# Sequence DFT summed apart over odd and even rows, and x loaded by row gathers, in an FNet-mixing and squared-ReLU kernel

## Chip, cores, metric

The kernel runs on one core of one Trainium2 chip. The metric is the device time of one execution, in microseconds (us). A "run" below is one kernel executed a few times beside the kernel before on the same chip. "Span" is the length of the one profiled execution, which is one or two us shorter than the time.

Engines are named as in the profile: PE (TensorE, the matmuls), DVE (VectorE), ACT (ScalarE), POOL (GpSimd) and SP (SyncE, which here only issues transfers, "DMAs"). SBUF is the on-chip memory, PSUM the one that the matmuls write.

## The reference

```python
x: (8, 3008, 256) f32;  w_in: (256, 2048);  w_out: (2048, 256)
X = fft(x, axis=1); X = fft(X, axis=2); a = X.real            # (8, 3008, 256)
h = maximum(a.reshape(-1, 256) @ w_in, 0)
return (h * h) @ w_out                                        # (24064, 256) f32
```

The real part of the two-dimensional DFT needs a cosine and a sine sum over the 3008 rows (the sequence DFT). Both kernels fold x first: rows n and 3008-n, n and 1504-n are added or subtracted, so that each sum runs over about 752 rows, held as 127 partitions times 6 values of q. The DFT over the 256 columns is multiplied into w_in once (G1, G2, G3).

## The kernel before: the parts that the change touches

x of one batch lies in one buffer. Half of it is needed in reversed row order. Eight large loads and two small ones go through the SP queue, which also carries the output stores and the edge rows:

```python
def down_rows(r0):                       # reversed half: slowest dimension is 3
    return bass.AP(tensor=x.tensor, offset=x.offset + r0 * D,
                   ap=[[PG * NQ * D, 3], [-NQ * D, PG], [1, NQ * D]])
def load_x(b):
    r = b * S
    for h in range(3):
        n0 = 1 + PG * NQ * (2 - h)
        for s in range(2):
            nc.sync.dma_start(out=x4[h*PG:(h+1)*PG, s, :, :], in_=up_rows(r + s*M + n0))
    for s in range(2):
        nc.sync.dma_start(out=x4[0:NP, 2 + s, :, :],
                          in_=down_rows(r + s*M + M - NQ - PG*NQ*2))
    ...                                  # two small loads of single rows
```

The 1505 frequencies of a batch are cut into four blocks. Every block takes 6 cosine and 6 sine matmuls (one for each q) of 376 columns, and 6 more for one "edge" row of features, done for one or two batches at a time:

```python
BLK = [(0, 377), (377, 376), (753, 376), (1129, 376)]
# one group, sn = 0 cosine, 1 sine:
mm(ps, w[0:KR, odd, q, :], cosT[0:KR, q, c0:c0+n], q == 0, q == NQ-1)     # x6
if q == NQ - 1:
    nc.scalar.copy(d[0:hi, c0:c0+n], ps[0:hi, :])
```

The main loop has 384 steps (48 chunks of 256 frequencies, 8 steps each). A step does 6 matmuls into xb (G1, G2, G3), two ReLUs on ACT, two squares on VectorE (DVE) and 8 matmuls of the previous chunk into po. The folds and the DFT of later batches are spread among the steps. In the profile lines xb and po are the PSUM tiles of the two products, r the ReLUs, h their squares, os output rows that wait to be stored, pt and qt the cosine and sine sums of a batch. The edge row is the cosine sum of the one feature (column 128) that the pairing of columns leaves over; it is made in tile es and copied by DMA into the last row of qt. Batch 0 is done ahead of the loop:

```python
alloc_pq(0); tables(0)
for f in fold_ops(0): f()                # ends with load_x(1)
gmats()
for f in stage1_ops(0, [0]) + e_ops([0], [0]): f()
for blk in (1, 2, 3):
    tables(blk)
    for f in stage1_ops(0, [blk]) + e_ops([0], [blk]): f()
```

## Time and profile before

| before | us |
|---|---|
| time, median of 3 | 832.75 (831.94 to 832.84) |
| span of the profiled run, mean granted clock | 831.6, 0.947 |
| first xb matmul (end of the head) | 98.6 |
| steps of batch 0 end (step 40) | 191.4 |

The last two rows come from the timeline of PE. They cut the span into three stages: the head (to the first xb matmul), batch 0's stage (40 steps, five chunks; the sixth already holds frequencies of batch 1) and the rest (344 steps).

The table by windows of the kernel before follows. The columns are the window and its length, then busy us (and instructions) of PE, PE weight loads, DVE, ACT and POOL, then the granted clock, the DMA share, and GB/s.

```profile
core 0: us, PE busy (x) PEld busy (x) DVE busy (x) ACT busy (x) POOL busy (x), PEclk, DMA share, GB/s
125.00:130.00 5.00, 5.00 (x44) 4.22 (x43) 0.00 (x0) 2.05 (x4) 0.00 (x0) 1.00 0.20 80
130.00:135.00 5.00, 0.57 (x6) 0.36 (x4) 0.00 (x0) 0.00 (x0) 0.00 (x0) 0.76 0.19 79
135.00:140.00 5.00, 0.00 (x0) 0.00 (x0) 2.02 (x5) 0.00 (x0) 0.00 (x0) 0.50 0.15 56
140.00:145.00 5.00, 4.32 (x20) 2.75 (x20) 5.00 (x13) 3.63 (x7) 0.00 (x0) 0.50 0.12 32
...
400.00:500.00 100.00, 98.42 (x925) 86.36 (x924) 51.50 (x138) 77.53 (x138) 0.00 (x0) 1.00 0.21 61
```

From 400 to 500 us PE is nearly always busy at full clock, so there PE is the bound. From 130 to 135 us no engine works for more than 0.6 us, while DMA moves only 79 GB/s at a share of 0.19, which is 3 of 16 engines. When PE starts again it has half the clock.

The timeline of the SP queue and of DVE, kernel before, shows what was awaited. Columns: start, us, engine, line, operation, tiles; in brackets the idle time before it and its releaser.

```profile
107.17 2.47 SPq L82 DMA_DIRECT2D x_96<-in_x_dram  x6
109.68 1.59 SPq L84 DMA_DIRECT2D x_96<-in_x_dram  x2
111.31 7.99 SPq L87 DMA_DIRECT2D x_96<-in_x_dram  x1
119.35 0.58 SPq L88 DMA_DIRECT2D x_96<-in_x_dram  x1
120.03 6.41 SPq L402 DMA_DIRECT2D out_dram<-os  x4
...
137.98 1.29 DVE L242 TENSOR_TENSOR u<-x_96 127x510 f16<-127x510 f32 x2 [14.31 <-DMA x_96<-in_x_dram]
```

x was asked for at 107.17 us and used at 137.98: 30.8 us for 3.08 MB. The small load at L87 held the queue for 8 us, and the stores (L402) stood behind it. During its 14.3 us wait for x DVE did nothing else. The squares that PE needs stand behind this fold in its program: they came at 139.2 us, ACT waited 12.6 us for them, and PE began again at 140.7.

### The profile page before, as it was taken

The page shows a single profiled execution, that of the slowest core. Times are in us where ns is not written, and L with a number is a line of the kernel's source. Part 1 is how long each engine was busy: PE and PEld are TensorE (multiplying, and loading weights), DVE is VectorE, ACT ScalarE, POOL GpSimd, SP SyncE. Part 2 cuts the span into 40 slices and gives each one's busy share as a digit, 9 for nine tenths or more (in the row PEclk, how much of TensorE's full clock was granted, in tenths as well). Part 3 has the DMA queues.
Part 4 walks back from the last instruction along what each step waited for, and adds up shares of the span by engine and source line. Part 5 has one row for each costly group of instructions (what it writes and reads, how often), then busy time and mean ns, then how long its engine had stood idle before and what let it go on. Part 6 is the DMA issues. An engine that isn't in the chain of part 4 may idle for free.

```text
span 831.6 us, 15590 instructions
## 1 busy us (share of the span) xinstructions
PE 709.7 (85%) x6200; PEld 580.1 (70%) x6200; DVE 403.7 (49%) x1097; ACT 558.6 (67%) x1008; POOL 11.4 (1%) x15
## 2 busy tenths in 40 slices
PE   0134595979999996979999995979999999999998
PEld 0012273848888975848888984847888988779887
DVE  3588573524444655423444655523444673334542
ACT  1535672746888864657778864646888887768884
POOL 5000000000000000000000000000000000000000
PEclk9995796989999997999999997989999999999999
DMA  9241041510111244311111243311111111101111
GB/s 176 72 111 41 2 115 68 139 63 32 39 39 39 72 119 114 107 42 39 39 39 39 63 122 108 113 49 39 34 44 40 40 39 39 36 29 41 51 39 52
DMA packets 35306, 52.57 MB, mean 63 GB/s; under 512 B 4034, under 2 KB 31202, under 8 KB 35234
## 3 DMA queue, kind: packets, MB, share of 16 engines
q1 hardware_dynamic: 32082, 49.49, 20.5%
q0 software_dynamic: 3152, 2.10, 1.8%
q8 instruction: 48, 0.79, 0.4%
q14 instruction: 24, 0.20, 0.1%
HBM read 29.00 MB, written 24.64 MB: 65 GB/s over the span
## 4 chain that ended last, share of the span: by engine, by line
PE 63%; DMA 18%; SPq 8%; DVE 7%; ACT 2%; issue 1%; POOL 1%; DVEq 0%; ACTq 0%; POOLq 0%
PE po L64 31%; PE xb L64 23%; DMA out_dram<-os 11%; DMA x_96<-in_x_dram 6%; PE pf L64 6%; SPq L87 4%; PE pe L64 3%; DVE u L242 2%; SPq L82 1%; SPq L84 1%; DVE tm L200 1%; DVE tt L203 1%; DMA qt<-es 1%; POOL x_96 L75 1%; SPq L88 1%
## 5 line engine op out<-in xcount | busy, mean ns | idle before, releaser
L435 ACT ACTIVATE r<-xb 128x512 f16<-128x512 f32 (+1 forms) x384 | 226.7, 591 | 134.3 <-PE xb L64 107.2
L446 ACT ACTIVATE r<-xb 128x512 f16<-128x512 f32 (+1 forms) x384 | 226.7, 590 | 25.4 <-PE xb L64 6.7
L64 PE MATMUL xb<-qt,G_199 128*128 128x256 f16 (+8 forms) x880 | 190.0, 259 | 2.0 <-DMA qt<-es 2.0
L64 PE MATMUL xb<-pt,G_198 128*128 128x256 f16 (+8 forms) x880 | 190.5, 260 | 0.6
L64 PE MATMUL xb<-qt,G_200 128*128 128x256 f16 (+8 forms) x880 | 148.4, 261 | 39.4 <-ACT r L435 39.4
L64 PEld LDWEIGHTS <-G_200 128*128 128x128 f16 x880 | 82.2, 99 | 50.4 <-issue 41.0
L64 PEld LDWEIGHTS <-G_198 128*128 128x128 f16 x880 | 83.9, 98 | 28.7 <-issue 16.9
L64 PEld LDWEIGHTS <-G_199 128*128 128x128 f16 x880 | 81.2, 98 | 19.7 <-issue 2.3
L376 ACT ACTIVATE os<-po 128x512 f32<-128x512 f32 (+1 forms) x95 | 56.3, 593 | 44.8 <-DMA out_dram<-os 40.8
L64 PE MATMUL pf<-cosT,w 127*128 127x376 f16 (+1 forms) x192 | 55.7, 344 | 24.0 <-ACT cosT L204 24.0
L64 PEld LDWEIGHTS <-w 127*127 127x127 f16 (+1 forms) x384 | 47.5, 126 | 39.5 <-issue 32.0
L64 PE MATMUL pf<-sinT,w 127*127 127x376 f16 (+1 forms) x192 | 55.2, 353 | 0.0
L242 DVE TENSOR_TENSOR u<-x_96 127x510 f16<-127x510 f32 x48 | 31.1, 685 | 46.5 <-DMA out_dram<-os 23.8
L64 PE MATMUL pe<-cosT,eall 127*2 127x376 f16 (+3 forms) x120 | 30.7, 361 | 9.4 <-ACT es L337 9.4
L64 PE MATMUL pc<-win_108,cosD 128*128 128x512 f16 x8 | 4.3, 615 | 30.7 <-DVE cosD L178 17.3
L204 ACT ACTIVATE cosT<-tt,bcos,tneg 128x376 f16<-128x376 f32 (+1 forms) x24 | 16.8, 699 | 15.4 <-DVE tt L203 15.4
L64 PEld LDWEIGHTS <-eall 127*2 127x2 f16 (+1 forms) x120 | 7.3, 86 | 24.4 <-issue 22.9
L64 PEld LDWEIGHTS <-cosD 128*128 128x128 f16 x8 | 1.0, 126 | 33.3 <-DVE cosD L178 19.4
L258 DVE TENSOR_TENSOR w<-v 127x381 f16<-127x381 f16 x64 | 20.7, 355 | 0.0
L311 ACT CAST qt<-pf 127x376 f16<-127x376 f32 (+1 forms) x32 | 15.3, 478 | 7.2 <-PE pf L64 7.2
L251 DVE TENSOR_TENSOR v<-u 127x512 f16<-127x512 f16 x48 | 18.6, 419 | 0.1
L311 ACT CAST pt<-pf 128x376 f16<-128x376 f32 (+1 forms) x32 | 15.4, 481 | 3.6 <-PE pf L64 3.4
(253 smaller groups left out, 1182.6 us busy)
## 6 DMA issues: line engine op xcount, KB each, us to landing
out_dram<-os SPq DMA_DIRECT2D x157, 128.0 KB
x_96<-in_x_dram SPq DMA_DIRECT2D x48, 252.0 KB
x_96<-in_x_dram SPq DMA_DIRECT2D x16, 756.0 KB
win_108<-in_moe_w_in_dram POOLq DMA_DIRECT2D x4, 256.0 KB, 13.8
wout_113<-in_moe_w_out_dram POOLq DMA_DIRECT2D x1, 1024.0 KB, 34.6
x_96<-in_x_dram SPq DMA_DIRECT2D x16, 2.0 KB
out_dram<-os SPq DMA_DIRECT2D x2, 108.0 KB
out_dram<-os SPq DMA_DIRECT2D x2, 104.0 KB
```

Of the source, the lines that this page charges most:

```text
L64: nc.tensor.matmul(o, l, r, start=start, stop=stop, skip_group_check=True)
L75: nc.gpsimd.memset(x4[96:128, :, :, :], 0.0)
L82: nc.sync.dma_start(out=x4[h * PG : (h + 1) * PG, s, :, :], in_=up_rows(r + s * M + n0))
L87: nc.sync.dma_start(out=t[:, 0 : NQ + 1 : NQ], in_=x[b : b + 1, 0 : M + 1 : M])
L204: nc.scalar.activation(cosT[:, q, c0 : c0 + n], t, AF.Sin, bias=bcos[:, q : q + 1], scale=tneg[:, q : q + 1])
L242: vt(u[k, :, q, 1:D], x4[k, 0:2, q, 1:D], x4[k, 3:1:-1, NQ - 1 - q, D - 1 : 0 : -1], op=ALU.add)
L251: vt(v[k, s, q : q + 2, :], u[k, 0, q : q + 2, :], u[k, 1, q : q + 2, :], op=ALU.subtract if s else ALU.add)
L258: vt(w[k, i, q : q + 3, 0 : P - 1], v[k, s, q : q + 3, 1:P], v[k, s, q : q + 3, D - 1 : P : -1], op=ALU.add if i < 2 else ALU.subtract)
L311: nc.scalar.copy(d[0:hi, c0 : c0 + n], ps[0:hi, :])
L376: nc.scalar.activation(os_[0:m, 0 : len(grp), :], st["o"][0:m, 0 : len(grp), :], AF.Copy, bias=0.0, scale=HS * HS)
L435: nc.scalar.activation(r[:, 0, :, 0:n], xb[:, :, 0:n], AF.Relu)
L446: nc.scalar.activation(r[:, 1, :, 0:n], xb[:, :, 0:n], AF.Relu)
```

## The change

The change has two parts and a new schedule that they allow.

1. For the lower half of the frequencies of each parity, odd and even rows are summed apart: A over even q, B over odd q. Then A+B is one frequency and the difference is its mirror image. So two blocks of 376 columns do the work of four. Each group costs 3+3 matmuls, one ACT copy of A to SBUF, and two DVE operations for sum and difference. Half the tables are needed. Edge rows are done for three and four batches at a time; those of batch 0 go into extra matmuls of its own groups.
2. x lies on the partitions in plain order; the reversed half is fetched by indirect DMA (a gather fetches 126 pieces of two rows, 2 KB each) on the GpSimd queue.
3. Only the first half of batch 0 is done ahead of the loop. The second half of its tables and its DFT go into steps 1 to 16, and the folds of batches 1, 2 and 3 into batch 0's steps.

```diff
+    def gather(b, s, part):
+        r0 = b * S + (s + 1) * M - NQ * NP + 2 * part
+        nc.gpsimd.indirect_dma_start(
+            out=x4[0:NP, 2 + s, 2 * part : 2 * part + 2, :].rearrange("p q d -> p (q d)"),
+            out_offset=None,
+            in_=bass.AP(tensor=x.tensor, offset=x.offset, ap=[[2 * D, B * S // 2], [1, 2 * D]]),
+            in_offset=bass.IndirectOffsetOnAxis(ap=idx[0:NP, 0:1], axis=0),
+            element_offset=r0 * D)
     def load_x(b):
-        ...                                     # 6 + 2 + 2 loads, nc.sync
         for s in range(2):
+            nc.gpsimd.dma_start(out=x4[0:NP, s, :, :], in_=up(b, s, 0, NQ))
+            for part in range(NQ // 2):
+                gather(b, 1 - s, part)
+        load_mid(b, nc.gpsimd)
-    BLK = [(0, 377), (377, 376), (753, 376), (1129, 376)]
+    BLK = ((0, HE), (HE, HO))                   # 377, 376 columns
...
+    # dft_ops: even q into one PSUM tile, odd q into another, then
+    act(st["a"], st[0], AF.Copy, ...)           # A to SBUF
+    vt(lo_, a, bp, op=ALU.add)                  # lower frequencies
+    vt(hi_, bp, a, op=ALU.subtract)             # mirrored ones (cosine)
...
-    alloc_pq(0) ... four rounds of tables, stage1, e_ops
+    for f in table_ops(0) + fe: f()             # fe: even half of the fold
+    for c in range(F // 512): gmat(c)
+    for f in stage1_ops(0, 0, True): f()
+    spread(fo, 1, 5)
+    spread(table_ops(1), 4, 10)
+    spread(stage1_ops(0, 1, True), 10, 16)
+    FOLD = {0: [1, 2, 3], 1: [4], 2: [5], 3: [6, 7]}
+    EGRP = {0: [1, 2, 3], 3: [4, 5, 6, 7]}
```

## The prediction

> **What bounds it now.** In undisturbed stretches PE does: the table by windows gives 400 to 500 us PE busy 98.4 of 100 us with 925 matmuls at clock 1.00, about 106 ns per 256-column matmul, so PE is at its rate; ACT is busy 78 us and DVE 52 us there. The rest is lost elsewhere. (a) The first xb matmul starts at 98.7 us (chain of waits): x is waited for until 40 us, then three rounds of tables, sequence DFT and edge DFT run in series. (b) Six pauses in which PE runs dry (about 130, 171, 310, 353, 501 and 541 us; roughly 43 us with the restarts, where the windows show clock 0.5). They come from x: the timeline of DVE shows it blocked 14.3 us before the fold at 138 us, and other chain pieces of 18 to 31 us are one x load landing. While the tail of a load arrives, the windows show a DMA share of 0.20 at 80 GB/s, about 3 of 16 engines. This agrees with the Trainium skill, "DMA: Bandwidth & Descriptors", section "Why a DMA increments its semaphore by 16 and not by 1": the engine count divides the slowest dimension, and the reversed load's slowest dimension is 3. The groups also show 6.8 us in issuing one small x row (L87), behind which output stores queue.
>
> **What the change does.**
> - Removes 276 matmuls of about 376 columns (192 sequence DFT, 84 edge DFT). At full rate one costs an estimated 0.16 us (from the 106 ns per 256 columns). 222 lie inside the PE-bound loop: -35 us.
> - Head: half the tables, no 5.2 us memset before x, x gathered by all engines, second half of the first batch's tables and DFT moved into the loop. Estimate: small vectors until 11 us, six table rounds of 2 us until 23, x by then, even folds (about 7 us) until 31, G and 18 DFT matmuls until 41. First xb at about 41 us: -57 us.
> - Adds per DFT group an ACT copy (half as many as before) and two VectorE sums of about 0.45 us (estimated from 0.41 to 0.61 us for 376-column f32 operations). ACT falls slightly, DVE rises some 10 to 15 us in all; neither becomes the bound in steady state (ACT 1.18 us of relus in a step of about 1.6 us).
> - Loads: 3.08 MB at the 187 GB/s seen when 16 engines run is 16.5 us (estimate), instead of about 31 us. Issue is off the store queue, onto an idle GpSimd.
> - New crowding: batch 0's steps now hold 12 us of tables and three folds. DVE there has an estimated 77 us of work in 40 steps, plus two waits of 4 to 8 us, as loads 2 and 3 are asked for only about 10 us ahead. So this stage is bound by DVE and x, ends at about 130 us (before: 194 us).
>
> **Sum.** 130 us to step 40; the remaining 344 steps took 638 us, of which about 37 are pauses; 600 - 33 (fewer matmuls) + 5 (batch 7's load) = 572. About 700 us; range 682 to 724. Chances: faster 0.97, same 0.02, slower 0.01.
>
> **What would show it.** First xb near 41 us; chunk 5 near 130; pauses after 150 us gone or under 5 us; 5924 matmuls, PE near 100% busy at clock 1.0, step about 1.65 us; x loads of 15 to 20 us with a DMA share well over 0.20; no long L87-like issues.
>
> **What would make it wrong.** Gathers slow to generate on GpSimd, or starved by DVE: each extra 10 us of load costs about 25 us in all. A loss of granted clock when PE has no pauses. Edge rows arriving late behind stores in the SP queue.

## More of the kernel before

Nor do the stores wait only for their turn. The waits of the SP queue (what waits, for what: us in all, times, longest) show that ten of them waited for an x load to land:

```profile
SPq L402 <- DMA x_96<-in_x_dram: 60.4, 10, 10.2
```

Three of PE's six pauses (5.4, 4.0 and 4.7 us, from 171, 353 and 542 us) begin in this way: DVE waits for no x there, but ACT waits 5.7 to 6.4 us for an output buffer that a late store holds.

## The result, and the profile after

The changed kernel takes 695.8 us (median of 4, 695.17 to 695.98) against 832.66 us before. The ratio is 0.8356, with a 95% interval of 0.8342 to 0.8371. A ratio is the mean time of one kernel's runs over that of the other's of the same rounds, so not quite the ratio of the medians quoted. The output is correct.

| span of the profiled run, us | before | predicted | after |
|---|---|---|---|
| head, to the first xb | 98.6 | 41 | 33.4 |
| batch 0's stage (40 steps) | 92.8 | 89 | 100.6 |
| rest (344 steps) | 640.2 | 572 | 559.4 |

The table by windows of the kernel after:

```profile
core 0: us, PE busy (x) PEld busy (x) DVE busy (x) ACT busy (x) POOL busy (x), PEclk, DMA share, GB/s
40.00:60.00 20.00, 8.90 (x48) 5.85 (x47) 14.89 (x40) 12.48 (x24) 0.00 (x0) 0.66 0.00 1
...
80.00:85.00 5.00, 2.31 (x21) 1.83 (x19) 0.00 (x0) 0.27 (x1) 1.84 (x3) 1.00 1.00 276
85.00:90.00 5.00, 0.00 (x0) 0.00 (x0) 2.40 (x5) 0.00 (x0) 0.00 (x0) 0.72 0.10 34
...
400.00:500.00 100.00, 100.00 (x947) 88.30 (x946) 52.63 (x136) 81.45 (x144) 0.00 (x0) 1.00 0.14 44
```

After step 40, until the last output stores, no 5 us window has PE idle for as much as 0.4 us; PE runs at clock 1.00 all the way. What remains is in batch 0's stage: a slow stretch from 40 to 60 us, and two pauses. The timeline of GpSimd (POOL) and of DVE, kernel after, shows the first pause:

```profile
67.94 0.53 POOL L116 DMA_DIRECT2D x_110<-in_x_dram  x1 [33.75 <-DVE u L259]
68.78 2.13 POOL L101 DMA_INDIRECT x_110<-in_x_dram,idx  x1 [0.30 <-issue]
71.20 1.02 POOL L101 DMA_INDIRECT x_110<-in_x_dram,idx  x1 [0.30 <-issue]
72.53 2.89 POOL L101 DMA_INDIRECT x_110<-in_x_dram,idx  x1 [0.31 <-issue]
...
81.29 0.56 POOL L112 DMA_DIRECT2D x_110<-in_x_dram  x1
...
87.60 1.89 DVE L255 TENSOR_TENSOR u<-x_110 127x510 f16<-127x510 f32 x3 [10.34 <-DMA x_110<-in_x_dram,idx]
...
109.10 1.29 DVE L255 TENSOR_TENSOR u<-x_110 127x510 f16<-127x510 f32 x2 [6.45 <-DMA x_110<-in_x_dram]
```

A load now takes 19.7 us (67.94 to 87.60), the next one 16.1 us, instead of 30.8. The two waits are 10.3 and 6.5 us.

### The profile page after: what moved, and what is told of

The parts are those of the page before. It is cut to its first block, busy times and chain, and to the rows that moved or that the text cites. A ratio compares the mean times of both kernels' runs of the same rounds, so it can differ in the third digit from the quotient of the medians.

```text
span 693.4 us, 14967 instructions
## 1 busy us (share of the span) xinstructions
PE 639.5 (92%) x5924; PEld 551.3 (80%) x5924; DVE 414.5 (60%) x1131; ACT 521.1 (75%) x936; POOL 79.6 (11%) x89
## 4 chain that ended last, share of the span: by engine, by line
PE 84%; DVE 6%; ACT 3%; POOL 2%; DMA 2%; issue 2%; DVEq 0%; ACTq 0%
PE po L74 46%; PE xb L74 34%; PE pf L74 5%; POOL x_110 L101 2%; DVE u L255 2%; DMA x_110<-in_x_dram,idx 1%; ACT sinT L216 1%; DMA x_110<-in_x_dram 1%; ACT cosT L219 1%; ACT r L460 1%; DVE tt L211 1%; DVE tm L214 1%; DVE tt L208 0%; ACT r L470 0%; DVE h_370 L474 0%
## 5 line engine op out<-in xcount | busy, mean ns | idle before, releaser
L101 POOL DMA_INDIRECT x_110<-in_x_dram,idx x48 | 59.5, 1240 | 14.5 <-issue 14.3
L255 DVE TENSOR_TENSOR u<-x_110 127x510 f16<-127x510 f32 x48 | 31.0, 683 | 16.8 <-DMA x_110<-in_x_dram,idx 10.3
L116 POOL DMA_DIRECT2D x_110<-in_x_dram x14 | 7.9, 566 | 217.9 <-DVE u L259 217.9
L74 PE MATMUL pf<-cosT,w 127*128 127x377 f16 (+1 forms) x96 | 30.1, 341 | 0.0
L74 PE MATMUL pf<-sinT,w 127*127 127x377 f16 (+1 forms) x96 | 29.8, 335 | 0.0
L74 PEld LDWEIGHTS <-w 127*128 127x128 f16 (+1 forms) x192 | 23.3, 122 | 3.9 <-issue 1.4
L74 PE MATMUL pc<-win_128,cosD 128*128 128x512 f16 x8 | 4.1, 614 | 19.7 <-DMA win_128<-in_moe_w_in_dram 17.9
L309 ACT ACTIVATE as<-pf 128x377 f32<-128x377 f32 (+7 forms) x34 | 16.6, 487 | 1.6 <-PE pf L74 1.4
L216 ACT ACTIVATE sinT<-tm,tsc 128x377 f16<-128x377 f32 (+1 forms) x12 | 6.8, 610 | 12.2 <-DVE tm L214 12.2
L74 PE MATMUL po<-wout_131,h_738 128*128 128x256 f16 x64 | 10.5, 291 | 0.0
```

The lines of the kernel that those rows point to most:

```text
L74: nc.tensor.matmul(o, l, r, start=start, stop=stop, skip_group_check=True)
L101: nc.gpsimd.indirect_dma_start(out=x4[0:NP, 2 + s, 2 * part : 2 * part + 2, :].rearrange("p q d -> p (q d)"), out_offset=None, in_=bass.AP ...
L116: nc.gpsimd.dma_start(out=x4[0:NP, s, :, :], in_=up(b, s, 0, NQ))
L216: act(sinT[:, q, cs], m[q], AF.Sin, bias=0.0, scale=tsc[:, q : q + 1])
L255: return lambda: vt(u[k, :, q, 1:D], x4[k, 0:2, q, 1:D], x4[k, 3:1:-1, NQ - 1 - q, D - 1 : 0 : -1], op=ALU.add)
L309: act(st["a"][0:m, :], st[0][0:m, :], AF.Copy, bias=0.0, scale=1.0) \
```

## The experiments

Ten kernels ran, each in 3 rounds, and all give correct results. The columns of this table are the median time, then the three stages of the profiled run.

| run | time | head | batch 0 | rest |
|---|---|---|---|---|
| before | 832.7 | 98.6 | 92.8 | 640.2 |
| changed | 695.8 | 33.4 | 100.6 | 559.4 |
| newdft_oldload | 781.2 | 52.3 | 126.4 | 600.4 |
| olddft_newload | 775.3 | 95.8 | 75.1 | 604.3 |
| newdft_load7 | 727.0 | 44.4 | 109.6 | 569.5 |
| mm_extra | 720.6 | 33.2 | 102.4 | 584.3 |
| x_double | 681.4 | 32.4 | 83.8 | 566.4 |
| gather_whole | 693.6 | 32.7 | 99.1 | 559.4 |
| spread_folds | 681.9 | 32.6 | 82.3 | 565.2 |
| spread_whole | 681.1 | 32.8 | 82.3 | 565.2 |
| tables_fine | 690.0 | 32.5 | 95.7 | 559.4 |
| spread_fine | 674.2 | 33.1 | 77.5 | 562.2 |

(The kernel before took 833.3 us in the rounds of the first four and of the last two runs, and 831.6 us in those of the other four. The stages add up to the span of the profiled execution, which is up to 3 us off the median: of the four executions it was the slowest in olddft_newload, mm_extra and x_double, and the fastest in newdft_load7.)

### newdft_oldload: undo the load path alone

```diff
-            nc.gpsimd.dma_start(out=x4[0:NP, s, :, :], in_=up(b, s, 0, NQ))
-            for part in range(NQ // 2):
-                gather(b, 1 - s, part)
-        load_mid(b, nc.gpsimd)
+        ...                    # the 6 + 2 loads of before, three row groups
+        load_mid(b, eng or nc.sync)
```

(The row numbers behind the tables follow the old row order; nothing else changes.)

> The changed kernel with only its load path undone: x again by 8 plain loads and two small ones per batch from the SP queue, with the old row order of three groups; the even/odd DFT, tables and schedule stay as changed. My theory (the load path and the DFT split are each worth tens of us, and nearly add up): x of batch 0 lands near 33 us instead of 20, first xb near 48 us (+15); the two waits of batch 0 and the one of batch 7 each grow by 10 to 14 us; in all about 749 us, 735 to 765. Rival 1 (the load path matters only for the first batch): about 711 us. Rival 2 (the load path is nearly all of the gain): above 790 us.

Measured: 781.2 us, outside the expected 735 to 765. The direction is that of the first theory, the size is not. x of batch 0 was used at 40.2 us, not near 33, and the two waits of batch 0 came to 21.3 us each. I had left out what else stands in the SP queue. The waits of PE and of the SP queue in this run (us in all, times, longest), and the window in the middle of the worst one:

```profile
PE xb L74 <- DMA qt<-es: 13.3, 1, 13.3
SPq L383 <- DMA x<-in_x_dram: 9.5, 1, 9.5
```

```profile
185.00:190.00 5.00, 0.00 (x0) 0.00 (x0) 0.00 (x0) 0.00 (x0) 0.00 (x0) 0.50 0.19 76
```

For 13.3 us PE waits for one edge row of 2.9 KB. The row was ready at 175.2 us, but its transfer (L383) was issued only at 190.4, after the loads of x and the stores ahead of it in the SP queue and after 9.5 us in which SP waited for an x load to land. Two more pauses, of 6.1 and 2.6 us, follow a store that comes late, so that ACT has no output buffer; another of 10.2 us is x of batch 7. So the load path was worth more than the wait for x: it also freed the queue for stores and edge rows.

### olddft_newload: the load path alone

```diff
-    nc.gpsimd.memset(x4[96:128, :, :, :], 0.0)
+    ...                        # idx, gather, load_x, load_mid as changed
-    nc.vector.tensor_scalar(out=nvec, in0=nvec, scalar1=adj[:, 0:1], ...)
```

> The kernel before with only the load path changed: row gathers and plain loads from the GpSimd queue, the new row order, no 5.2 us memset; DFT, tables and schedule as before. My theory: the first xb moves little (about 94 us instead of 98.7, as the tables still run in series), but the six pauses of about 43 us nearly vanish; about 790 us, 778 to 802. Rival 1 (pauses come from something else): 825 us or more. Rival 2 (the load path is nearly all of the gain): below 760 us.

Measured: 775.3 us, a little better than the expected 778 to 802. The head hardly moves (95.8 us): the tables and DFT of batch 0 still run in series. Batch 0's stage loses 17.7 us and the rest 35.9 us, which agrees with the 37 us of pauses that the prediction had read there. One caution: here the index rows of the tables stand behind the gathers on GpSimd, and DVE began at 17.3 us instead of 11.8, so the head could be up to 5 us shorter.

With the two runs, the parts alone give 52 us (DFT and schedule) and 58 us (loads); together they give 137. The 27 us between come mainly from the head (16 of them): its cut is 46.3 us with the new DFT alone, 2.8 with the new loads alone, and 65.2 with both. An early x is worth something only when the tables no longer run in series behind it, and a short head only when x is there.

### newdft_load7: seven row groups instead of three

```diff
-                       ap=[[PG * NQ * D, 3], [-NQ * D, PG], [1, NQ * D]])
+                       ap=[[PG * NQ * D, G], [-NQ * D, PG], [1, NQ * D]])   # G = 7
```

(The first line is that of newdft_oldload. The other half of x comes in 14 small loads instead of 6.)

> As newdft_oldload, but with seven row groups instead of three, so that the slowest dimension of the reversed load is 7. If the old loads are slow because only three DMA engines carry the reversed half (my theory), seven carry it at about 175 GB/s (an estimate from 80 GB/s on three), a load takes about 18 us, and the time comes within 12 us of the changed kernel's 696 us: 690 to 712. Rival (reading rows in reverse order, or the SP queue, is slow in itself): like newdft_oldload, about 749 us. In the trace I expect a DMA share near 0.45 in the tail of a load instead of 0.20.

Measured: 727.0 us, between the two theories, 54 us faster than with three groups. In the tail of one load, the windows of the run with three groups and of the run with seven:

```profile
106.00:111.00 5.00, 0.00 (x0) 0.00 (x0) 0.00 (x0) 0.00 (x0) 0.00 (x0) 0.50 0.19 79
```

```profile
93.00:98.00 5.00, 0.22 (x3) 0.05 (x1) 0.00 (x0) 0.00 (x0) 0.00 (x0) 0.96 0.44 182
```

The share went from 0.19 to 0.44, which is 3 and 7 of 16 engines, and the rate from 79 to 182 GB/s. So the count of engines is why the reversed half moved slowly, not the reversed order and not the queue, which are the same in both runs. This agrees with the Trainium skill, "DMA: Bandwidth & Descriptors", section "Why a DMA increments its semaphore by 16 and not by 1". The two loads of batch 0's stage still took 22.2 and 22.4 us (7 us of it issue of 14 small loads), and one edge row still came 6.0 us late behind loads in the SP queue; hence 727 and not 696.

### mm_extra: give matmuls back

```diff
                 hi, wt, q, tab = mms(par)[i]
+                if i == 0 and looped:
+                    for _ in range(3):
+                        mm(st[par][0:hi, :], wt(q), tab[k, q, c0 : c0 + n], True, False)
```

> The changed kernel with 180 extra matmuls of 376 columns in the loop: the first matmul of every DFT group there is issued four times (each restarts the sum, so the result stays right). It gives back on PE most of what the split saves in the loop, and nothing else. My theory (the loop is bound by PE at about 0.157 us per such matmul, but some 48 of the extra ones fall into batch 0's steps, which VectorE and x bound): +20 to +29 us, about 721 us. Rival (the loop is bound by ACT or VectorE, and the removed matmuls were not the gain): less than +8 us.

Measured: 720.6 us, +24.8 us, as the theory said. The count of 180 in the expectation was a miscount: the edge groups got extra matmuls too, and the profile has 6128 matmuls against 5924, so 204 more. The stages say where the time is. In the rest there are 156 of them (24 for each of batches 2 to 7, and 12 of an edge group); it grew by 24.9 us, 0.160 us each. In batch 0's stage there are 48 (12 of batch 0's odd half, 24 of batch 1, 12 of an edge group); it grew by 1.8 us in all, because there PE is not the bound.

### x_double: two buffers for x

```diff
-    x4 = xp.tile([P, 4, NQ, D], F32, name="x4")
+    x4s = [xp.tile([P, 4, NQ, D], F32, name=f"x4{i}") for i in range(2)]
...
-        if b + 1 < B: ops.append(lambda: load_x(b + 1))
+        if b + 2 < B: ops.append(lambda: load_x(b + 2))
```

(To make room, there are three output buffers instead of four; no wait of ACT for a store is among this run's longer waits. The load of batch 1 is issued before the loop.)

> The changed kernel with two buffers for x, so that each batch's load is asked for one fold earlier (output staging cut from four buffers to three to make room). The two waits for x in batch 0's steps (10.3 and 6.5 us on VectorE) go, with no other work changed. My theory (VectorE's wait for x is what makes batch 0 longer than I had estimated, and each wait costs PE nearly its length and a restart at half clock): batch 0's stage falls from 100.6 to about 82 us and the whole to about 677 us, 672 to 682. Rival (batch 0 is bound by VectorE's and ACT's own work, and the waits only fill slack): at least 688 us.

Measured: 681.4 us (679.3 to 684.5). Batch 0's stage is 83.8 us, 16.8 us less, as much as the 10.3 + 6.5 us of waits. So nearly none of those waits filled slack, and the rival falls. In the profiled execution, the slowest of the four, the rest is 7 us longer; its waits show why:

```profile
PE xb L74 <- DMA qt<-es: 3.9, 1, 3.9
```

An edge row came 3.9 us late at the seam of batch 0 and 1, and PE ran at half clock for 5.6 us after it began again, which costs about 2.8 us more (an estimate). That makes 6.7 of the 7 us.

### gather_whole: two gathers instead of six

```diff
-            for part in range(NQ // 2):
-                gather(b, 1 - s, part)
+            gather6(b, 1 - s)              # 126 pieces of 6 rows, 6 KB each
```

> The changed kernel with the reversed half loaded by one gather of 6-row pieces per half instead of three gathers of 2-row pieces (all loads but the first batch's and the last one of all), so GpSimd makes 2 gathers per batch instead of 6, for the same bytes. In the changed kernel GpSimd took 13.9 and 11.7 us to issue the two loads that VectorE waited for. Theory A (a load is bound by the issue on GpSimd, about 1.3 us a gather and up to 2.9 us beside VectorE's work): a load takes 12 to 14 us instead of 16 to 20, the two waits shrink to 5 us in sum, about 685 us. Theory B (a load is bound by the transfer): same time as the changed kernel within 3 us, 693 to 699.

Measured: 693.6 us; theory B. GpSimd needed 5.9 and 6.8 us to issue the two loads instead of 13.9 and 11.7, and yet they took 16.8 and 16.5 us instead of 19.7 and 16.1. The waits were 7.4 and 6.9 us. So issue on GpSimd lengthened the first of the two loads by about 3 us, and the transfer bounds them otherwise: in the middle of that load the DMA share was 0.63 in the changed kernel (73 to 78 us) and 1.00 here (72 to 77 us). This rests on one profile of each, and the pieces are larger here. But mm_extra and tables_fine, which make the six gathers, fit: 11.5 and 12.9 us of issue went with loads of 16.1 and 17.1 us.

### spread_folds, spread_whole: move two folds out of batch 0

```diff
-    FOLD = {0: [1, 2, 3], 1: [4], 2: [5], 3: [6, 7]}
-    EGRP = {0: [1, 2, 3], 3: [4, 5, 6, 7]}
+    FOLD = {0: [1], 1: [2, 3], 2: [4], 3: [5], 4: [6], 5: [7]}
+    EGRP = {0: [1], 1: [2, 3], 3: [4, 5], 5: [6, 7]}
```

(The folding in batch 0's steps is also set to end sooner, and batch 1 starts the DFT of batch 2 later, so that each fold is done before its use. spread_whole has gather_whole in it too.)

> The changed kernel with the folds of batches 2 and 3 moved from batch 0's steps to batch 1's (and each later fold one batch before its use; edge rows in four groups instead of two, which adds 24 matmuls, about 4 us). My theory: batch 0's stage loses 18 us of VectorE work and both waits and falls from 100.6 to about 74 us; batch 1 takes the work without a pause, as PE has 77 us of its own there; about 674 us, 668 to 682. Rival (batch 1 then pauses for x instead, the gain is only moved): 688 us or more.

> spread_folds and gather_whole together. If spread_folds leaves no wait for x, this gains nothing over it (within 2 us); if a wait for batch 3's x is left in batch 1's steps, this takes it away, 2 to 6 us.

Measured: 681.9 us and 681.1 us. No DVE wait for x is among the longer waits any more, and gather_whole on top gains nothing. But batch 0's stage is 82.3 us, not 74: I had counted DVE's work only, and forgotten that its first ten steps are slow for another reason; the next runs take 4.8 of these 8.3 us back. The 24 extra edge matmuls cost more than I had said: the rest grew by 5.8 us, 0.24 us each instead of 0.16. (That is an estimate, as folds moved too; spread_fine agrees, with 12 extra edge matmuls and +2.8 us in the rest, 0.23 us each.) The timeline of PE in the changed kernel shows where it comes from; first a step with three edge matmuls, then one without:

```profile
126.10 0.60 PE L74 MATMUL po<-wout_131,h_956 128*128 128x256 f16 x4
126.63 0.64 PE L74 MATMUL pf<-cosT,eall 127*3 127x376 f16 x3
127.20 0.28 PE L74 MATMUL xb<-pt,G_198 128*128 128x256 f16 x1
...
130.51 0.60 PE L74 MATMUL po<-wout_131,h_956 128*128 128x256 f16 x4
130.95 0.27 PE L74 MATMUL xb<-pt,G_198 128*128 128x256 f16 x1
```

From start to start, the four po matmuls take 0.53 us where edge matmuls follow and 0.44 us where not; the three edge matmuls take 0.57 us. The single start times of the rest, in the same trace, take this apart. An edge matmul that another one follows takes 0.159 us, no more than a wide one. The last of a run takes 0.255 us, and the po matmul before the run 0.202 instead of 0.109. So the extra comes where PE changes from weights of 128 columns to weights of 1 to 4 and back: about 0.2 us for each run of two or three. Five runs hold 12 edge matmuls, and 0.16 + 0.2 x 5/12 makes 0.24 us.

### tables_fine, spread_fine: do not let DVE and ACT wait for each other

```diff
-    spread(table_ops(1), 4, 10)            # two q at once: 8 DVE, 4 ACT operations
+    spread(fine_table_ops(1), 3, 10)       # DVE for q, ACT for q - 1, in each step
```

> The changed kernel with the second half of the first batch's tables issued one q per step, and their two ACT sines one step after the VectorE work they need (before: two q at once, in steps 4, 6, 8). In the changed kernel each pair took 6.44 us for two steps, with VectorE waiting 1.6 us for ACT and ACT for VectorE, PE busy 8.9 of 20 us. Theory (the two engines wait for each other because both run in program order): steps 3 to 10 take about 2.6 us each, the fold of batch 1 starts 3 to 4 us earlier, the whole 692 us, 690 to 694. Rival (bound by VectorE's work alone): no change, 695 to 697.

> spread_folds plus tables_fine, with the last four edge rows in one group again (12 matmuls fewer, -2 us): the version that the runs point to. If the gains add: 682 - 4 - 2 = 676 us, 673 to 679.

Measured: 690.0 us, at the lower edge of what was expected, and 674.2 us, within it. The timeline of DVE in the changed kernel and in spread_fine, around the tables:

```profile
47.75 0.74 DVE L208 TENSOR_SCALAR tt<-krow,nfrac 128x376 f32<-128x376 f32 x2
...
50.89 0.42 DVE L472 TENSOR_TENSOR h_370<-r 128x512 f16<-128x512 f16 x1
52.88 0.43 DVE L474 TENSOR_TENSOR h_370<-r 128x512 f16<-128x512 f16 x1 [1.56 <-ACT r L470]
53.22 0.42 DVE L472 TENSOR_TENSOR h_370<-r 128x512 f16<-128x512 f16 x1
53.85 0.42 DVE L474 TENSOR_TENSOR h_370<-r 128x512 f16<-128x512 f16 x1 [0.21 <-ACT r L470]
54.19 0.73 DVE L208 TENSOR_SCALAR tt<-krow,nfrac 128x376 f32<-128x376 f32 x2
```

```profile
48.09 0.41 DVE L233 TENSOR_SCALAR tt<-krow,nfrac 128x376 f32<-128x376 f32 x1
...
50.04 0.42 DVE L503 TENSOR_TENSOR h<-r 128x512 f16<-128x512 f16 x1
50.37 0.42 DVE L505 TENSOR_TENSOR h<-r 128x512 f16<-128x512 f16 x1
50.71 0.41 DVE L233 TENSOR_SCALAR tt<-krow,nfrac 128x376 f32<-128x376 f32 x1
```

Before, two steps took 6.44 us (47.75 to 54.19), with DVE idle 1.77 us: a square waits for a ReLU, the ReLU stands behind four sines on ACT, and the sines wait for DVE. Now one step takes 2.62 us with DVE never idle. Of the 4.9 us that batch 0's stage loses in tables_fine, 3.1 lie before the fold of batch 1 (it begins 26.7 us after the first xb instead of 29.7); the rest goes with a first load of 17.1 instead of 19.7 us. The cleaner pair is spread_fine and spread_folds, in which no fold waits long for x: the stage is 4.8 us shorter, all of it before that fold (26.7 instead of 31.4). spread_fine is the fastest kernel that ran: ratio 0.8097 to the kernel before (0.8082 to 0.8112).

## Why the prediction was right, point by point

The total, 700 us against 695.8, was right, and so in the main was the cause of each large part. But the three stages missed by -7.6, +11.6 and -12.6 us. That the total still came out within about 1% is partly luck.

- **PE bounds the loop; 0.16 us a matmul.** Right. mm_extra measured 0.160 us. The rest then ran without pauses at full clock, as foretold.
- **"600 - 33 (fewer matmuls) + 5 (batch 7's load) = 572."** The rest was 559.4. The pauses were sized right: olddft_newload loses 35.9 us there against 37. (The way was only half named. "They come from x" holds for all six, but three of them reach PE through late stores and not through DVE's wait; see the profile before.) Batch 7's load did not delay anything, so the +5 falls. And the DFT part was worth 44.9 us (604.3 to 559.4), not 33. The term that was mis-sized is the edge DFT: of the 204 matmuls taken out of the rest, 60 were edge ones, and spread_folds priced those at 0.24 us. 144 x 0.16 + 60 x 0.24 makes about 37.4 us (an estimate from these two runs). In olddft_newload PE also waited 4.0 us in all for its single edge PSUM tile and 1.9 us for edge rows at seams, waits that the changed kernel does not have. That accounts for about 43 of 44.9 us. No run of its own tests it, but the start times of PE's matmuls in the two traces add up to nearly the same: from olddft_newload to the changed kernel the matmuls of the main DFT take 23.1 us less, the edge matmuls with their waits 16.7, those of xb 2.7 and those of po 2.2.
- **"First xb at about 41 us."** It came at 33.4. The small vectors were done at 7.7 us instead of 11, because their index rows are now first on GpSimd; and x was there when the tables ended at 20 us, as said. DVE did not wait for x at all. That the gain needs both parts of the change (65.2 us against 46.3 and 2.8) was not foreseen.
- **"This stage is bound by DVE and x, ends at about 130 us."** It ended at 134.0, and from a head 8 us shorter, so this stage was 11.6 us longer than predicted (100.6 against 89). "Two waits of 4 to 8 us" were 10.3 and 6.5 us, and x_double shows that they cost their full 16.8 us. The DVE sum of 77 us was not too low: DVE was busy 72.7 us there, and with the two waits that makes 89.5. What the sum missed is the other 11.1 us in which DVE is idle, 7.8 of them before the fold of batch 1, where DVE and ACT wait for each other over the tables; spread_fine takes 4.8 us of that back.
- **"Loads: ... 16.5 us (estimate)."** Measured 16.1 and 19.7 us. The longer one is 3 us of slow issue on GpSimd; that risk was named, and it was small (gather_whole).
- **Three engines for the reversed half.** Right; newdft_load7 shows it by moving the number.
- **"Edge rows arriving late behind stores in the SP queue"** was named as a risk. It did not happen in the changed kernel, but in newdft_oldload it cost 13.3 us in one place.

Why a pause costs more than itself: the Trainium skill, "TensorE: Matmul & The Clock Gate", Part 1, says that the array falls back to half its clock after an idle stretch of about 3.4 us. The windows agree as to the half: clock 0.50 from 135 to 145 us before, 0.72 in the window of the first pause after. As to the time they agree only roughly: the clock fell 2.0 us after PE's last matmul before (at 132.6 us), and 4.9 us after it in the changed kernel (at 87.2 us). It stayed at half for another 5.6 and 3.1 us after PE had begun again.

## What to carry to other kernels

Split the span into stages at events that both kernels have, and predict each stage. Here three errors of 8 to 13 us hid behind a total that was right within about 1%. When loads share a queue with small transfers that an engine awaits, price the queue too: in newdft_oldload, stores and edge rows held up behind x cost 22 us of pauses (13.3, 6.1 and 2.6). Even a transfer that is ready can wait there for a large one to land (9.5 us in newdft_oldload). And look at the slowest dimension of an access pattern before blaming its direction.

## What the Trainium skill lacked or had wrong

- "DMA: Bandwidth & Descriptors", section "Anatomy of one DMA — SWDGE (gpsimd) path", gives 2.0 us plus bytes over 436 GB/s for a DMA. Applied to the 3.08 MB of one batch that makes about 9 us (an estimate from that page); the loads took 16.1 to 19.7 us in ten DMAs, beside output stores. The best 5 us window that was looked at in a load of the changed kernel (305 to 310 us) had 291 GB/s, at a DMA share of 1.03. The page has nothing on the rate or the issue time of indirect DMAs.
- Issue of one gather of 126 pieces takes GpSimd 0.98 us at best; no page has this for an indirect DMA. In places it took far longer: 2.89 us in the changed kernel, 6.78 us in x_double, 7.23 us in olddft_newload. In x_double VectorE ran additions and squares back to back through nearly the whole of it. "SBUF — State Buffer", section "Who interferes with whom", says that a VectorE instruction with two SBUF inputs contends with a GpSimd instruction that reads SBUF. A gather reads its row numbers there, so this could fit. But a busy VectorE is not enough: in the changed kernel another gather, with VectorE busy throughout, took 1.02 us (at 118.19). No run here shows the cause.
- "TensorE: Matmul & The Clock Gate", section "Back-to-back issue gap", gives N/2.4 + 2.5 ns, which makes 159 ns for 376 columns (an estimate from that page), but as the gap of an isolated matmul: in a stream of weight loads and matmuls, it says, the formula gives too much at large N. Here it held in such a stream: mm_extra's matmuls, each with its own weight load, took 0.160 us.
- No page gives a time for the change between wide and narrow weights. It cost about 0.2 us for each run of edge matmuls (spread_folds); why, no run here shows.
